# Batch 0's k and q transposed head by head, memory values cast by the DMA, and three x copies moved to ScalarE, in a chunked-attention and snake-MLP kernel

## The chip, the cores and the metric

The kernel runs on one core of a Trainium2 chip. The metric is the device time of one execution in microseconds; where several executions are shown, the median is meant. The profile is of one further execution, and its times are counted from the start of its span. Engines are named as in the profile: PE is TensorE (PEld its weight loads), DVE is VectorE, ACT is ScalarE, POOL is GpSimd, SP is SyncE.

## The reference

Two stages follow one another: a chunked attention with memory tokens over 4 batches, 8 heads, 768 positions and a head size of 64, and a two-layer MLP over the 3072 tokens that come out of it.

```python
def _attn_ref(q, k, v, mem_k, mem_v):           # q, k, v: (4, 8, 768, 64); mem: (4, 8, 8, 64)
    chunk, left_ctx, right_ctx = (32, 16, 8)
    scale = 1.0 / np.sqrt(D)
    for c in range(S // chunk):
        l_start, r_end = max(0, 32 * c - 16), min(S, 32 * c + 32 + 8)
        q_c = q[:, :, 32 * c:32 * c + 32]
        k_full = np.concatenate([mem_k, k[:, :, l_start:r_end]], axis=2)
        v_full = np.concatenate([mem_v, v[:, :, l_start:r_end]], axis=2)
        a = softmax(scale * np.matmul(q_c, k_full.transpose(0, 1, 3, 2)))
        out[:, :, 32 * c:32 * c + 32] = np.matmul(a, v_full)

def _moe_ref(x, w_in, w_out, alpha):            # x: (3072, 512), w_in: (512, 2048), w_out: (2048, 512)
    h = x @ w_in
    s = np.sin(alpha * h)
    g = h + s * s / (alpha + 1e-09)
    return g @ w_out
```

All inputs and the output are float32; the kernel multiplies in bfloat16.

## The kernel before, in words

**Tiling.** A batch has 8 blocks of 96 queries (`QW`), each three chunks of 32. A block's keys and values are a window of 128 rows: 120 of the sequence and 8 of the memory, which sit at rows 64 to 71 of the window. `kTi` holds the transposed keys of a batch with the memory keys put in between the blocks, `qT` the transposed queries, and the two tiles `vws` the values of two successive batches with a column of ones, which gives the sums for the softmax. The mask is in the bias of the exponential (`biasm`).

**Loading.** k and q come by DMA from POOL's queue, cast to bfloat16, with six successive positions in one partition, so a row moved is long. Batch 0 is loaded by pairs of heads (`load_qk_pair`, eight DMAs), later batches whole (`load_qk`). Because of the six positions, transposing a pair of heads takes six transposes of 128 by 128. `pair_up` (L226) first copies a pair of heads so that the two heads' 64 columns lie side by side for each of the six; `t_k` and `t_q` transpose that copy into PSUM and copy the result to `kTi` on VectorE (L243, and two short ones at L249) and to `qT` on ScalarE (L258). v of batch 0 is loaded by blocks, two DMAs each (`load_v`, L125 and L129), later batches by four large DMAs (`load_v_all`, L139 to L148). The memory values are loaded in float32 from SP's queue, cast on ScalarE (L418), and spread over the eight blocks of a batch by `put_memv` (L153), a VectorE copy of 4096 elements on 8 partitions. POOL's DMA issues take turns on eight semaphores; each waits until the DMA that used its semaphore before has landed.

**The order of work** is written out by hand (`manual_schedule`): each engine runs its instructions in the order of the program.

1. *The opening* (L412 to L438): for batch 0, k and q of the four pairs of heads in turn are regrouped, transposed and copied out. `spin` puts filler matmuls of zeros on TensorE (L171): ten at the start, two after each of the eight tiles. Then come `put_memv(0)` and the issue of all weights, of batch 1's k and q, of w_out and of batch 1's v.
2. *The burst* of a batch (`burst`): for block s, the scores are multiplied (L266) and three exponentials taken on ScalarE (`qk_exp`, L275); `lag` steps later the values are multiplied (L288), and VectorE takes the reciprocal (L292) and scales (L293, `x_blk`); one step after that the block is transposed (L306) and copied into `xT` (`xt`, L309). In batch 0 each step also has one filler matmul, and the transposes have a PSUM tile of their own; in later batches second-layer matmuls of the batch before fill the gaps.
3. *The first layer* (`l1`): for each of 16 feature tiles ft, eight matmuls of 384 columns (L341), a sine on ScalarE (L353), its square on ScalarE (L356), VectorE (L362) or POOL (L358) as a string of letters says, and on VectorE gT = square x inverse alpha + h (L370, or L366 where a tile is split). For batch 0 the letters are `ADADADAAADADADAA`: VectorE squares ft 1, 3, 5, 9, 11 and 13. `put_memk(1)` and `put_memv(1)` stand ahead of it.
4. *The second layer* (`l2`, L398) of a batch, interleaved with the next batch's opening and burst, and then the loop goes on.

Tile pools decide who waits for buffers: scores, attention outputs and first-layer outputs share three PSUM tiles (`big`), fillers and transposes two (`smp`).

Of the kernel before, what the change touches and what calls it, by code (L numbers as in the profile page):

```python
# [9 lines left out]
P = 128  # L10
QW = 96
# [3 lines left out]
F32 = mybir.dt.float32  # L15
# [30 lines left out]
def kernel(  # L46
# [12 lines left out]
    nc = tc.nc  # L59
    B, H, S, D = q.shape  # L60
# [3 lines left out]
    NJ = S // QW  # L64
    HP = H // 2
# [8 lines left out]
    gp = ctx.enter_context(tc.tile_pool(name="gp", bufs=2))  # L74
# [8 lines left out]
    ident = consts.tile([P, P], BF, name="ident")  # L83
# [7 lines left out]
    memkT = consts.tile([P, HP, 32], BF, name="memkT")  # L91
    memv_st = consts.tile([P, B, H, D], BF, name="memv_st")
    memk_f = gp.tile([32, H, D], F32, name="memk_f", tag="gT")
    memv_f = gp.tile([P, B, H, D], F32, name="memv_f", tag="gT")
    w_in_sb = consts.tile([P, KT, d_ff], BF, name="w_in_sb")
    w_out_sb = consts.tile([P, FT, d_model], BF, name="w_out_sb")
    alpha_sb = consts.tile([P, FT], F32, name="alpha_sb")
# [9 lines left out]
    def alloc_qk():  # L107
        kb = qkst.tile([P, H, 6, D], BF, name="k_bf")
        qb = qkst.tile([P, H, 6, D], BF, name="q_bf")
        return kb, qb  # L110

    def load_qk(b):
        kb, qb = alloc_qk()
        for src, dst in ((k, kb), (q, qb)):
            nc.gpsimd.dma_start(
                dst[:].rearrange("p h r d -> p h (r d)"),
                src[b].rearrange("h (p r) d -> p h (r d)", p=P),
            )
        return kb, qb
# [30 lines left out]
            vf.rearrange("(n p) d -> p n d", p=QW)[0:8, 1:n])  # L150

    def put_memv(b):
        nc.vector.tensor_copy(  # L153
            vws[b % 2][64:72, :, :, 0:D],
            memv_st[64:72, b].unsqueeze(2).to_broadcast([NM, H, NJ, D]),
        )

    def put_memk(b):
        nc.vector.tensor_copy(
            kTi[:, :, 24:KW].rearrange("p g (j c) -> p g j c", c=104)[:, :, :, 40:40 + NM],  # L160
            memkT[:, :, NM * b:NM * b + NM].unsqueeze(2).to_broadcast([P, HP, NJ, NM]),
        )
# [4 lines left out]
    def spin(n):  # L167

        z = smp.tile([P, 512], F32, name="z", tag="sm")
        for _ in range(n):  # L170
            nc.tensor.matmul(z[:], zeros[:, 0:P], zeros[:])  # L171
# [8 lines left out]
    kq = alloc_qk()  # L180
# [3 lines left out]
        load_qk_pair(0, hp, *kq)  # L184
    for b in range(B):
        nc.sync.dma_start(memk_f[NM * b:NM * b + NM], mem_k[b].rearrange("h n d -> n h d"))
    nc.sync.dma_start(memv_f[64:72].rearrange("n b h d -> n (b h) d"),
                      mem_v.rearrange("b h n d -> n (b h) d"))
    nc.gpsimd.memset(biasm[:], NEG)
    nc.gpsimd.memset(biasm[:, 0:1], 0.0)  # L190
    for c0, c1, thr, val in (
# [16 lines left out]
    for pt in pts:  # L208
        nc.vector.memset(pt[:, H * QW:H * QW + 32], 0.0)

    def load_w_in(c):
        nc.gpsimd.dma_start(
            w_in_sb[:, :, 256 * c:256 * c + 256],
            moe_w_in[:, 256 * c:256 * c + 256].rearrange("(kt p) f -> p kt f", p=P),
        )

    def load_w_out(c):
        nc.gpsimd.dma_start(
            w_out_sb[:, 4 * c:4 * c + 4, :],
            moe_w_out[512 * c:512 * c + 512].rearrange("(ft p) o -> p ft o", p=P),  # L220
        )


    def pair_up(src, hp, eng=None):
        pr = blk.tile([P, 6, 2, D], BF, name="pr")
        (eng or nc.gpsimd.tensor_copy)(  # L226
            pr[:].rearrange("p r e d -> p e r d"), src[:, 2 * hp:2 * hp + 2]
        )
        return pr
# [3 lines left out]
    def t_tile():  # L233
        state["t"] += 1
        if state["t"] % state["pools"] == 0:
            return smp.tile([P, 6, P], BF, name="tt_a", tag="sm")
        return big.tile([P, 6, P], BF, name="tt_b", tag="big")

    def t_k(kb, hp):
        t = t_tile()  # L240
        for r in range(6):
            nc.tensor.transpose(t[:, r, :], kb[:, r].rearrange("p e d -> p (e d)"), ident[:])  # L242
        nc.vector.tensor_copy(  # L243
            kTi[:, hp, 72:72 + 7 * 104].rearrange("p (s c) -> p s c", c=104)[:, :, 0:96]
            .rearrange("p s (a r) -> p s a r", r=6),
            t[:, :, 8:120].rearrange("p r (s a) -> p s a r", a=16),
        )
        for t0, c0 in ((0, 16), (120, 800)):
            nc.vector.tensor_copy(  # L249
                kTi[:, hp, c0:c0 + 48].rearrange("p (a r) -> p a r", r=6),  # L250
                t[:, :, t0:t0 + 8].rearrange("p r a -> p a r"),
            )

    def t_q(qb, hp):
        t = t_tile()
        for r in range(6):
            nc.tensor.transpose(t[:, r, :], qb[:, r].rearrange("p e d -> p (e d)"), ident[:])  # L257
        nc.scalar.copy(  # L258
            qT[:, hp, :].rearrange("p (a r) -> p a r", r=6), t[:].rearrange("p r a -> p a r")
        )  # L260

    def qk_exp(j):
        sc = big.tile([P, 2, 512], F32, name="sc", tag="big")
        for hp in range(HP):
            for e in range(2):
                nc.tensor.matmul(  # L266
                    sc[:, e, QW * hp:QW * hp + QW],
                    kTi[64 * e:64 * e + 64, hp, 104 * j:104 * j + P],
                    qT[64 * e:64 * e + 64, hp, QW * j:QW * j + QW],
                )  # L270
        pt = pts[state["n"] % NPT]
        state["n"] += 1
        for m in range(3):
            col = ((1 if j == 0 else 0), 4, (3 if j == NJ - 1 else 2))[m]
            nc.scalar.activation(  # L275
                pt[:, 0:H * QW].rearrange("p (g e c) -> p e g c", g=4, e=2)[:, :, :, 32 * m:32 * m + 32],
                sc[:, :, 0:4 * QW].rearrange("p g (e c) -> p g e c", e=4)[:, :, :, 32 * m:32 * m + 32],
                ACTF.Exp, bias=biasm[:, col:col + 1], scale=0.125,
            )
        return pt  # L280
# [19 lines left out]
    def xt(xT, j, x_blk, ot):  # L300
        if ot is None:
            xtp = smp.tile([P, KT, QW], BF, name="xtp", tag="sm")[:]
        else:
            xtp = ot[:].bitcast(BF)[:, 0, 640:640 + KT * QW].rearrange("p (k c) -> p k c", k=KT)
        for kt in range(KT):
            nc.tensor.transpose(  # L306
                xtp[:, kt, :], x_blk[:, 2 * kt:2 * kt + 2, :].rearrange("p e d -> p (e d)"), ident[0:QW, 0:QW]
            )
        nc.vector.tensor_copy(xT[:, :, QW * j:QW * j + QW], xtp)  # L309

    def burst(b, stream, shares, lag):

        xT = xp.tile([P, KT, S], BF, name="xT")
        ptl, xbl = {}, {}
        for s in range(NJ + lag + 1):
            n = shares[s] if s < len(shares) else 0
            if s < NJ:
                ptl[s] = qk_exp(s)
            if b == 0:
                spin(1)  # L320
            stream.take(n // 3, True)
            if 0 <= s - lag < NJ:
                xbl[s - lag] = pv(b, s - lag, ptl.pop(s - lag))
                if b == 0:
                    xbl[s - lag] = (xbl[s - lag][0], None)
            stream.take((n + 1) // 3, True)
            if 0 <= s - lag - 1 < NJ:
                xt(xT, s - lag - 1, *xbl.pop(s - lag - 1))
            stream.take((n + 2) // 3, True)
        return xT  # L330

# [77 lines left out]
            yield True  # L409


    first = [nc.vector.tensor_copy, nc.scalar.copy] * 2 + [nc.vector.tensor_copy] * 4  # L412
    prs = [pair_up(kq[n], 0, first[n]) for n in range(2)]
    for n in range(2 * HP):
        (t_k if n % 2 == 0 else t_q)(prs[n], n // 2)
        spin(2)
        if n == 3:
            nc.scalar.copy(memv_st[64:72], memv_f[64:72])  # L418
        if n == 1:
            mt = smp.tile([P, HP, 32], BF, name="mt", tag="sm")  # L420
            for hp in range(HP):
                nc.tensor.transpose(
                    mt[:, hp, :],
                    memk_bf[0:32, 2 * hp:2 * hp + 2, :].rearrange("p e d -> p (e d)"),
                    ident[0:32, 0:32])
        if n + 2 < 2 * HP:
            prs.append(pair_up(kq[n % 2], (n + 2) // 2, first[n + 2]))
        if n == 1:
            nc.vector.tensor_copy(memkT[:], mt[:])
            put_memk(0)  # L430
    put_memv(0)
    nc.vector.reciprocal(inv_alpha[:], alpha_sb[:])
    for c in range(8):
        load_w_in(c)
    kq_next = load_qk(1)
    for c in range(4):
        load_w_out(c)
    load_v_all(1)  # L438

# [1 line left out]
    xT = burst(0, stream, (), 2)  # L441
# [3 lines left out]
    for i in range(B):  # L445
        gT = gp.tile([P, FT, S], BF, name="gT")
# [31 lines left out]
        if not last:  # L478
# [8 lines left out]
            if i == 0:  # L487
                xT = burst(i + 1, stream, (3, 3, 3, 4, 4, 4, 4, 4, 4, 4, 5, 5), 3)
            else:
                xT = burst(i + 1, stream, (16, 8, 6, 6, 6, 5, 5, 5, 5, 5), 1)  # L490
# [37 lines left out]
```

The softmax here doesn't subtract the row's maximum and nothing guards it: scores larger than these inputs give would overflow.

## Time and profile before

| | us |
|---|---|
| median of 10 runs | 237.34 |
| lowest and highest of them | 236.68, 239.56 |
| the profiled execution | 239.56 |
| its span (first to last instruction) | 237.8 |
| TensorE, VectorE, ScalarE, POOL busy | 220.9, 160.5, 153.7, 72.9 |
| opening, until the first exponential (L275) | 0 to 18.50 |
| burst of batch 0, until the first layer's matmuls run on | 18.50 to 30.75 |
| first layer of batch 0 | 30.75 to 58 |
| TensorE at half clock within it | 30.9 to 34.3 |

The busy times are sums over the whole span. Every batch goes through the same stages, but the first 58 us differ from the rest: there is no second layer of an earlier batch to fill TensorE, so other engines and the DMA set the pace, and the sums over the whole span say little about that stretch. It is read by the chain of waits and by the busy time of each engine in short stretches.

### The profile page before, as it was taken

The numbers are of one execution on the slowest core, as the hardware profiler recorded it, in microseconds if no ns is written. First come the engines' busy times: TensorE is split into PE (matmuls) and PEld (weight loads), VectorE is DVE, ScalarE is ACT, GpSimd is POOL, SyncE is SP. The second block draws the span as 40 slices with busy tenths as digits, with TensorE's granted clock in tenths as the row PEclk, the third lists the DMA queues.
The fourth block names the chain that finished last, engine by engine and source line by source line (L and its number), as shares of the span: only waits on it lengthen the run. The fifth ranks groups of instructions, "written<-read, shape, count | busy, mean of one in ns | idle before, by whom it ended". The sixth has DMA issues, their size and how long they took to land.

```text
span 237.8 us, 4467 instructions
## 1 busy us (share of the span) xinstructions
PE 220.9 (93%) x1759; PEld 124.3 (52%) x1785; DVE 160.5 (67%) x287; ACT 153.7 (65%) x237; POOL 72.9 (31%) x96
## 2 busy tenths in 40 slices
PE   7798899989989999998999999998999999899994
PEld 2455546545535566565455565664455555453453
DVE  3376949899717886998656688978556367875110
ACT  2569839995497358798766597779564675971000
POOL 7899874302662022409320115120000010020000
PEclk9999979999999999999999999999999999999999
DMA  6999999999999920016999101001111110101122
GB/s 77 150 147 82 149 192 203 206 207 129 113 197 182 141 77 3 0 45 78 199 154 137 44 3 44 3 0 44 47 44 47 45 44 3 44 0 44 50 85 88
DMA packets 53852, 21.11 MB, mean 89 GB/s; under 512 B 36296, under 2 KB 50888, under 8 KB 53832
## 3 DMA queue, kind: packets, MB, share of 16 engines
q0 software_dynamic: 47616, 14.40, 77.0%
q1 hardware_dynamic: 6216, 6.43, 9.4%
q8 instruction: 14, 0.23, 0.4%
q14 instruction: 6, 0.05, 0.1%
HBM read 28.91 MB, written 6.29 MB: 148 GB/s over the span
## 4 chain that ended last, share of the span: by engine, by line
PE 63%; DVE 12%; ACT 11%; issue 6%; DMA 3%; POOL 3%; POOLq 1%; DVEq 0%; ACTq 0%
PE o L398 29%; PE hT L341 22%; DVE gT L370 5%; ACT pt L275 4%; ACT u L353 3%; DMA q_bf<-in_q_dram 3%; PE ot L288 3%; PE sc L266 3%; DVE s L362 2%; PE ot L306 2%; DVE x_blk L293 2%; PE o L387 1%; ACT s L356 1%; POOL k_bf L102 1%; PE tt_a L257 1%
## 5 line engine op out<-in xcount | busy, mean ns | idle before, releaser
L398 PE MATMUL o<-w_out_sb,gT 128*128 128x512 bf16 x343 | 93.1, 380 | 2.0 <-issue 0.5
L341 PE MATMUL hT<-xT,w_in_sb 128*128 128x384 bf16 x488 | 89.0, 330 | 3.8 <-DVE gT L370 3.3
L370 DVE SCALAR_TENSOR_TENSOR gT<-s,inv_alpha,hT 128x768 bf16<-128x768 f32 x61 | 60.9, 1012 | 22.8 <-ACT s L356 14.8
L353 ACT ACTIVATE u<-hT,alpha_sb 128x768 f32<-128x768 f32 x61 | 54.6, 898 | 27.0 <-PE hT L341 26.0
L341 PEld LDWEIGHTS <-w_in_sb 128*128 128x128 bf16 x512 | 49.9, 99 | 39.6 <-issue 6.4
L275 ACT ACTIVATE pt<-sc,biasm 128x256 bf16<-128x256 f32 x96 | 37.5, 492 | 12.5 <-PE sc L266 12.5
L398 PEld LDWEIGHTS <-gT 128*128 128x128 bf16 x368 | 31.8, 97 | 26.2 <-DVE gT L370 1.2
L358 POOL TENSOR_TENSOR s<-u 128x768 f32<-128x768 f32 x6 | 8.8, 1466 | 71.6 <-ACT u L353 61.3
L356 ACT ACTIVATE s<-u 128x768 f32<-128x768 f32 x34 | 28.7, 843 | 1.1
L362 DVE TENSOR_TENSOR s<-u 128x768 f32<-128x768 f32 x24 | 24.8, 1033 | 0.7 <-ACT u L353 0.5
L226 POOL COPY pr<-q_bf 128x768 bf16<-128x768 bf16 x12 | 10.1, 838 | 43.7 <-PE tt_a L242 26.1
L293 DVE TENSOR_TENSOR x_blk<-ot,rinv 96x512 bf16<-96x512 f32 x32 | 22.0, 686 | 1.1
L292 DVE RECIPROCAL rinv<-ot 96x8 f32<-96x8 f32 x32 | 6.5, 202 | 20.0 <-PE ot L288 19.6
L407 ACT COPY o_sb<-o 128x512 f32<-128x512 f32 x11 | 6.4, 585 | 20.0 <-PE o L398 20.0
L405 DVE COPY o_sb<-o 128x512 f32<-128x512 f32 x12 | 8.2, 687 | 15.4 <-PE o L398 15.1
L171 PE MATMUL z<-zeros 128*128 128x512 bf16 x36 | 14.9, 502 | 1.3 <-DVE zeros L165 1.3
L288 PEld LDWEIGHTS <-pt 128*128 128x128 bf16 x256 | 11.9, 98 | 7.2 <-issue 2.3
L266 PEld LDWEIGHTS <-kTi 64*128 64x128 bf16 x256 | 7.0, 94 | 13.3 <-issue 6.8
L288 PE MATMUL ot<-vw,pt 128*128 128x65 bf16 x256 | 13.0, 193 | 0.9 <-ACT pt L275 0.6
L266 PE MATMUL sc<-qT,kTi 64*128 64x96 bf16 x256 | 11.4, 205 | 2.2 <-ACT pt L275 1.2
L306 PEld LDWEIGHTS <-x_blk 96*128 96x128 bf16 x128 | 8.4, 97 | 6.6 <-DVE x_blk L293 1.5
L242 PEld LDWEIGHTS <-pr 128*128 128x128 bf16 x96 | 6.9, 103 | 6.4 <-DVE pr L226 3.2
(66 smaller groups left out, 183.0 us busy)
## 6 DMA issues: line engine op xcount, KB each, us to landing
out_dram<-o_sb SPq DMA_DIRECT2D x23, 256.0 KB, 2.6
k_bf<-in_k_dram POOLq DMA_DIRECT2D x3, 768.0 KB, 8.1
q_bf<-in_q_dram POOLq DMA_DIRECT2D x3, 768.0 KB, 11.4
vw<-in_v_dram POOLq DMA_DIRECT2D x6, 384.0 KB, 17.3
w_in_sb<-in_moe_w_in_dram POOLq DMA_DIRECT2D x8, 256.0 KB, 8.0
w_out_sb<-in_moe_w_out_dram POOLq DMA_DIRECT2D x4, 512.0 KB, 18.7
k_bf<-in_k_dram POOLq DMA_DIRECT2D x4, 192.0 KB, 6.5
q_bf<-in_q_dram POOLq DMA_DIRECT2D x4, 192.0 KB, 6.7
```

The lines of the kernel that those rows point to most:

```text
L171: nc.tensor.matmul(z[:], zeros[:, 0:P], zeros[:])
L266: nc.tensor.matmul(sc[:, e, QW * hp:QW * hp + QW], kTi[64 * e:64 * e + 64, hp, 104 * j:104 * j + P], qT[64 * e:64 * e + 64, hp, QW * j:QW ...
L275: nc.scalar.activation(pt[:, 0:H * QW].rearrange("p (g e c) -> p e g c", g=4, e=2)[:, :, :, 32 * m:32 * m + 32], sc[:, :, 0:4 * QW].rearra ...
L288: nc.tensor.matmul(otv[:, h // 4, h % 4, :], pt[:, QW * h:QW * h + P], vws[b % 2][:, h, j, 0:D + 1])
L293: nc.vector.tensor_tensor(out=x_blk[:].rearrange("p (g e) d -> p g e d", g=2), in0=otv[0:QW, :, :, 0:D], in1=rv.unsqueeze(3).to_broadcast( ...
L306: nc.tensor.transpose(xtp[:, kt, :], x_blk[:, 2 * kt:2 * kt + 2, :].rearrange("p e d -> p (e d)"), ident[0:QW, 0:QW])
L341: nc.tensor.matmul(hts[hf][:, 0:HALF], w_in_sb[:, kt, P * ft:P * ft + P], xT[:, kt, HALF * hf:HALF * hf + HALF], start=(kt == 0), stop=(kt ...
L353: nc.scalar.activation(u[:], hT[:, :, 0:HALF], ACTF.Sin, scale=alpha_sb[:, ft:ft + 1])
L356: nc.scalar.activation(s2[:], u[:], ACTF.Square)
L362: nc.vector.tensor_tensor(out=s2[:], in0=u[:], in1=u[:], op=ALU.mult)
L370: nc.vector.scalar_tensor_tensor(out=gv, in0=s2[:], scalar=inv_alpha[:, ft:ft + 1], in1=hT[:, :, 0:HALF], op0=ALU.mult, op1=ALU.add)
L398: nc.tensor.matmul(o[:], gT[:, ft, P * s:P * s + P], w_out_sb[:, ft, :], start=(ft == 0), stop=(ft == FT - 1),)
```

## The change

- In the opening the regrouping copies are gone. A new function `turn` transposes straight from the loaded tile: for each of the six positions two transposes of one head's 64 columns, into the upper and the lower 64 partitions of the PSUM tile. (For batches 1 to 3 it works on the regrouped tile as before.) After each tile there is one filler matmul instead of two.
- The memory values are loaded by a DMA from POOL's queue, issued behind the eight of k and q, that casts to bfloat16. The DMA on SP's queue and the cast on ScalarE are gone.
- `put_memv(0)` stands after the fifth of the eight tiles instead of after the last. `put_memv(1)` runs on POOL instead of VectorE; batches 2 and 3 stay on VectorE.
- w_in is loaded by five DMAs (256, 256, 512, 512, 512 columns) instead of eight of 256, and w_out by two instead of four.
- In batch 0's burst a block is transposed and copied into `xT` two steps after its values are multiplied instead of one (`back`), which makes the burst one step longer; the copies of blocks 5, 6 and 7 run on ScalarE.

```diff
@@ tiles, put_memv, loads
-    memv_f = gp.tile([P, B, H, D], F32, name="memv_f", tag="gT")
...
     def put_memv(b):
-        nc.vector.tensor_copy(
+        (nc.gpsimd if b == 1 else nc.vector).tensor_copy(
             vws[b % 2][64:72, :, :, 0:D],
...
-    nc.sync.dma_start(memv_f[64:72].rearrange("n b h d -> n (b h) d"),
-                      mem_v.rearrange("b h n d -> n (b h) d"))
+    nc.gpsimd.dma_start(memv_st[64:72].rearrange("n b h d -> n (b h) d"),
+                        mem_v.rearrange("b h n d -> n (b h) d"))
...
-    def load_w_in(c):
+    def load_w_in(c0, c1):
         nc.gpsimd.dma_start(
-            w_in_sb[:, :, 256 * c:256 * c + 256],
-            moe_w_in[:, 256 * c:256 * c + 256].rearrange("(kt p) f -> p kt f", p=P),
+            w_in_sb[:, :, c0:c1],
+            moe_w_in[:, c0:c1].rearrange("(kt p) f -> p kt f", p=P),
         )
     def load_w_out(c):
         nc.gpsimd.dma_start(
-            w_out_sb[:, 4 * c:4 * c + 4, :],
-            moe_w_out[512 * c:512 * c + 512].rearrange("(ft p) o -> p ft o", p=P),
+            w_out_sb[:, 8 * c:8 * c + 8, :],
+            moe_w_out[1024 * c:1024 * c + 1024].rearrange("(ft p) o -> p ft o", p=P),
         )
@@ transposes
-    def t_k(kb, hp):
+    def turn(src, hp):
         t = t_tile()
         for r in range(6):
-            nc.tensor.transpose(t[:, r, :], kb[:, r].rearrange("p e d -> p (e d)"), ident[:])
+            if src.shape[1] == 6:
+                nc.tensor.transpose(t[:, r, :], src[:, r].rearrange("p e d -> p (e d)"), ident[:])
+            else:
+                for e in range(2):
+                    nc.tensor.transpose(t[64 * e:64 * e + 64, r, :], src[:, 2 * hp + e, r, :], ident[:])
+        return t
+
+    def t_k(kb, hp):
+        t = turn(kb, hp)
...
     def t_q(qb, hp):
-        t = t_tile()
-        for r in range(6):
-            nc.tensor.transpose(t[:, r, :], qb[:, r].rearrange("p e d -> p (e d)"), ident[:])
+        t = turn(qb, hp)
@@ xt, burst
-        nc.vector.tensor_copy(xT[:, :, QW * j:QW * j + QW], xtp)
+        (nc.scalar.copy if ot is None and j >= 5 else nc.vector.tensor_copy)(
+            xT[:, :, QW * j:QW * j + QW], xtp)
...
-        for s in range(NJ + lag + 1):
+        back = lag + (2 if b == 0 else 1)
+        for s in range(NJ + back):
...
-            if 0 <= s - lag - 1 < NJ:
-                xt(xT, s - lag - 1, *xbl.pop(s - lag - 1))
+            if 0 <= s - back < NJ:
+                xt(xT, s - back, *xbl.pop(s - back))
@@ the opening
-    first = [nc.vector.tensor_copy, nc.scalar.copy] * 2 + [nc.vector.tensor_copy] * 4
-    prs = [pair_up(kq[n], 0, first[n]) for n in range(2)]
     for n in range(2 * HP):
-        (t_k if n % 2 == 0 else t_q)(prs[n], n // 2)
-        spin(2)
-        if n == 3:
-            nc.scalar.copy(memv_st[64:72], memv_f[64:72])
+        (t_k if n % 2 == 0 else t_q)(kq[n % 2], n // 2)
+        spin(1)
         if n == 1:
...
-        if n + 2 < 2 * HP:
-            prs.append(pair_up(kq[n % 2], (n + 2) // 2, first[n + 2]))
-        if n == 1:
             nc.vector.tensor_copy(memkT[:], mt[:])
             put_memk(0)
-    put_memv(0)
+        if n == 4:
+            put_memv(0)
     nc.vector.reciprocal(inv_alpha[:], alpha_sb[:])
-    for c in range(8):
-        load_w_in(c)
+    for c0, c1 in ((0, 256), (256, 512), (512, 1024), (1024, 1536), (1536, 2048)):
+        load_w_in(c0, c1)
     kq_next = load_qk(1)
-    for c in range(4):
+    for c in range(2):
         load_w_out(c)
     load_v_all(1)
```

## The prediction

> **What bounds the kernel now.** I read the page first, for the busy shares and the forty slices.
>
> ```profile
> PE 220.9 (93%) x1759; PEld 124.3 (52%) x1785; DVE 160.5 (67%) x287; ACT 153.7 (65%) x237; POOL 72.9 (31%) x96
> PEclk9999979999999999999999999999999999999999
> ```
>
> TensorE is busy nearly throughout, but the change touches only the first 60 us, and those have limits of their own: one slice (29.7 to 35.7 us) shows a lower clock. Next, the chain of waits over 0 to 62 us.
>
> ```profile
> 7.08 7.51 DMA q_bf<-in_q_dram
> ...
> 15.59 0.38 DVE pr L226
> ...
> 16.02 0.51 PE tt_b L242 x6
> ...
> 17.33 0.81 ACT qT L258
> ...
> 18.50 5.58 ACT pt L275 x15
> ...
> 29.21 0.70 DVE x_blk L293
> ...
> 29.96 0.36 PE xtp L306 x4
> ...
> 30.34 0.37 DVE xT L309
> ...
> 30.75 5.58 PE hT L341 x23
> ```
>
> Three stages: **the opening** (to 18.50) ends when the last q has landed (7.08 + 7.51 = 14.59), been regrouped, transposed and copied to qT; **the burst** of batch 0 (18.50 to 30.75) is set by the exponentials, then by VectorE; **the first layer** of batch 0 follows. The third view, busy time by stretch, shows what limits that layer.
>
> ```profile
> 27.44:30.86 3.42, 2.22 (x27) 1.24 (x25) 3.17 (x11) 1.27 (x1) 2.28 (x4) 1.00 1.24 161
> ...
> 32.00:33.00 1.00, 1.00 (x5) 0.48 (x4) 0.06 (x1) 0.00 (x0) 1.00 (x2) 0.50 1.48 194
> ...
> 50.00:55.00 5.00, 3.87 (x24) 2.21 (x24) 4.96 (x8) 4.39 (x6) 0.00 (x0) 1.00 1.46 194
> ```
>
> The columns are PE, PEld, DVE, ACT and POOL busy, then the clock. At 32 us TensorE runs at half clock and VectorE is idle; from 36 to 57 us VectorE is busy 19.8 of 21.0 us. Whatever holds VectorE there moves the end. The timeline gives the rows that I price with.
>
> ```profile
> 17.68 1.27 DVE L153 COPY vw<-memv_st 8x4096 bf16<-8x4096 bf16 x1
> ...
> 39.11 0.96 DVE L362 TENSOR_TENSOR s<-u 128x768 f32<-128x768 f32 x1
> ...
> 45.46 0.83 POOL L148 DMA_DIRECT2D vw<-in_v_dram  x1 [3.14 <-DMA q_bf<-in_q_dram]
> ...
> 87.88 1.49 DVE L362 TENSOR_TENSOR s<-u 128x768 f32<-128x768 f32 x1
> ```
>
> The same square takes 0.96 us at 39.11 and 1.49 at 87.88, where a POOL copy (L226, 87.74 to 88.57) lies over its start.
>
> [...] the two squares under a POOL copy end 0.81 us after it (1.49 and 1.37 us against 0.95), while L370, with one SBUF input, stays at 1.01 under such copies. [...] Here it reads 0.50 at 31 to 34 us, after 2.22 busy of 3.42; matmuls of L341 start 0.32 us apart there and 0.163 later. [...]
>
> **The change, part by part.**
>
> *Opening.* Eight regrouping copies go (VectorE six, 0.34 to 0.52 us each; ScalarE two of 0.83), and ScalarE's cast of the memory values (1.90 us at 14.35). TensorE gets 12 transposes of 64 columns for 6 of 128, and one filler matmul for two. A transpose starts every 0.107 us at half clock, 0.056 at full; a filler takes 0.427 or 0.214. If half transposes go one by one, a tile costs 12 x 0.107 + 0.43 = 1.71 us cold, 0.89 warm (before: 1.50, 0.76); if the two column halves run side by side, 1.07 and 0.55. Tiles land about every 1.0 us, so only the cold serial case queues.
> What is late next is the memory values. Their DMA leaves the SP queue for POOL's, behind the eight k and q loads, and lands after the last q: 14.6 to 15.1 (the v load behind them now lands at 10.13 + 4.97 = 15.1). The copy that spreads them (L153, 1.27 us) moved from behind the last k copies to ahead of them on VectorE. So VectorE waits to about 14.9, spreads until 16.2, then evacuates the last k (0.86 + 0.31) until 17.4; before it finished at 17.65 and qT at 18.13. ScalarE's last qT is ready by 16.7. The first exponential starts at about 17.8 for 18.50: **0.7 us gained**. Bounds: 1.3 if SP's lighter queue lands everything 0.5 us sooner; 0 if cold, serial transposes delay the last k to 16.8 on VectorE.
>
> *Burst.* Copying x one step later and the last three on ScalarE takes 3 x 0.34 us from VectorE, but not from the path. After the second x_blk VectorE has no free time; before, copies 1 to 5 stand between it and the last x_blk (copy 0 fell into a wait), after it copies 0 to 4: five each time. After the last x_blk, before: 29.90 to 30.70. After: transposes 0.4, then a ScalarE copy of 384 elements, about 0.48 on the line through its 512 (0.585, L407) and 768 (0.80, L258): 0.9. **0.1 lost** (bounds -0.3, +0.2). The Sine table load (1.28 us, now right after the exponentials) follows these copies and still fits under the first layer's first matmuls (1.3 us or more). One more filler on TensorE is under VectorE's work.
>
> *POOL's queue.* One DMA issue more before the v loads (0.7 us), less the 0.36 us for which the first of them waits beside a regrouping copy: first-layer weights start 0.4 us later, v still lands 1.5 us or more before its use. The spread of batch 0 holds up one v load (1.34 us for 0.7) before and after alike. The 8 weight issues become 5 and the 4 of w_out 2; rows of twice the length should move like k's (768 KB in 3.9 us) instead of w_in's 256 KB in 1.5, so w_in is complete at 21.9 + 0.4 + 4.8 + 1.5 + 3 x 2.6 = 36.4 (before 27.1 + 10.3 = 37.4). Nothing on the chain waits for weights; the first w_out matmul is at 55.1, and the second half, due about 55.5, is first read at 57.6. Nothing gained or lost; were that slack of 2 us gone, each further microsecond of delay would pass to the end.
>
> *The spread of batch 1.* put_memv(1) leaves VectorE (1.22 us at 30.84, in time that VectorE idles until 34.92: nothing gained) and goes to POOL, queued behind the last v load. A POOL DMA issue waits for the landing of the eighth before it (L148 above waits for q, eight earlier); for that v load this is now the last w_in. It issues at 36.7, until 37.4; then POOL copies 4096 elements. POOL's copies of 768 take 0.83 us, so 4.4 us[...]. I take 4.4[...]. The square of ft 3, due at 39.11 - 0.6 = 38.5, then ends 0.81 after POOL at 42.6 instead of 39.5: 3.1 late, and behind it on VectorE wait all gT of the layer, and so TensorE for PSUM. VectorE has one 0.53 us gap at 46.3 and some 0.2 of small ones to take this up; I count **2.2 lost**[...]. If the layer starts 1.3 sooner at full clock, the square of ft 5 is hit instead, for about as much.
>
> *Sum:* -0.7 + 0.1 + 2.2 = **+1.6 us**. The profiled execution took 239.56 (span 237.8 and 1.8 around it), the highest of the ten; the sum on it gives 241.2. Its half clock at the layer's start, some 1.3 us, may be part of its 2.2 above the median; I put the sum on the median: 237.34 + 1.6 = 238.9.
>
> **Rivals.** *The POOL copy stalls nothing* (not slower): it is done in under 1.1 us, or lies outside every square; L370, which it can't hold, fills half of VectorE's time. Then -0.6: 236.7. Against it: squares come every 3 us[...]. It decides where POOL's copy takes under 1.1 us.
> *That, and TensorE stays at full clock* into the first layer, since the tail of the burst gets one more filler (0.21 of 3.4 us): eight matmuls at 0.163 for 0.325, another -1.3: 235.4. For it: 2.22 of 3.42 us was the only stretch that dropped. Against it: the addition is small.
> *The clock falls earlier.* Eight fillers fewer leave TensorE cold into the burst: a step then costs about 1.5 us against the exponentials' 1.07, for one 3.4 us window: +1.5 on the sum, 240.4. Against it: cold, the doubled transposes fill the time anyway.
> That the change doesn't act is excluded: copies and DMAs are gone from the program.
>
> **The numbers.** Likeliest case 0.48, stall-free 0.23, stall-free and warm 0.22, cold 0.07. Hence faster by over 0.5% (1.2 us, about what a measurement of this kernel can tell from none) 0.22, within it 0.23, slower 0.55. The likeliest gives 238.9, its own range 237.9 to 239.9; the others and the unknown prices stretch it to 235.8 to 240.9.
>
> **What would show it.** Right: put_memv on POOL at about 37[...], and one L362 of 2.5 us or more under it; first exponential at 17.2 to 18.3, with L153 ahead of the last L243 of the opening; last x_blk to first-layer matmul 0.9 us. Wrong: L362 at 0.95 throughout, or POOL's copy under 1.1 us; or an exponential before 17, if the memory values land ahead of the last q.

## The result, and the profile after

| | before | after |
|---|---|---|
| median (us) | 237.21 | 240.23 |
| lowest, highest of the runs (us) | 235.85, 239.56 | 238.49, 243.40 |
| ratio to before, with its 95% interval | | 1.0100 (1.0072 to 1.0128) |
| profiled execution (us), its span | 239.56, 237.8 | 238.68, 237.0 |

The kernel became slower, by 3.0 us in the medians over all runs and by 1.0% (2.4 us) in the ratio, which leaves out a few disturbed executions. The two profiled executions stand the other way round: after's is near its own low end, and before's was the highest of its ten. The profile therefore has to be read for what happens in it, not for its end time. First the page of after: the busy row of the engines and the granted clock by slices.

```profile
PE 218.1 (92%) x1800; PEld 123.3 (52%) x1826; DVE 157.7 (67%) x277; ACT 151.8 (64%) x237; POOL 73.1 (31%) x93
PEclk9797999999999999999999999999999999999999
```

VectorE's work fell by 2.8 us (160.5 before), as the removed and moved copies let one expect, and yet nothing was won. The clock row now dips twice, in slices 2 and 4 (5.9 to 11.9 and 17.8 to 23.7 us), where that of before dipped at 29.7 to 35.7. The chain of waits of after, in order of time, shows the stages.

```profile
7.79 7.06 DMA memv_st<-in_mem_v_dram
14.88 1.22 DVE vw L152
16.11 0.86 DVE kTi L251
17.13 0.24 PE sc L272 x2
17.45 2.31 ACT pt L281 x6
...
29.82 0.49 ACT xT L315
30.35 3.90 PE hT L349 x23
...
39.88 0.92 DVE gT L378
40.80 2.18 DVE s L370
...
57.16 0.85 DVE kTi L251
```

The opening now ends with the memory values, as the prediction had it: their DMA (7.79 + 7.06 = 14.85), the spread `put_memv(0)` (L152), the last k copy, and only then the scores and the first exponential at 17.45. The other new item is a square (L370) of 2.18 us on the chain. The timeline shows what lies over it.

```profile
37.75 0.95 DVE L370 TENSOR_TENSOR s<-u 128x768 f32<-128x768 f32 x1
38.36 3.79 POOL L152 COPY vw<-memv_st 8x4096 bf16<-8x4096 bf16 x1
...
40.72 2.25 DVE L370 TENSOR_TENSOR s<-u 128x768 f32<-128x768 f32 x1
...
44.14 2.76 PE L349 MATMUL hT<-xT,w_in_sb 128*128 128x384 bf16 x16 [1.61 <-DVE gT L378]
```

`put_memv(1)` on POOL runs from 38.36 to 42.15. The square that falls into it ends at 42.97, 0.82 after POOL, having taken 2.25 us for its usual 0.95; TensorE then waits 1.61 us for a gT. The third view, busy time by stretch, has the columns PE, PEld, DVE, ACT and POOL busy, then the clock.

```profile
14.86:18.28 3.42, 1.52 (x23) 0.72 (x24) 2.56 (x5) 1.49 (x4) 3.42 (x5) 1.00 1.30 79
18.28:21.69 3.41, 3.27 (x42) 2.15 (x43) 1.21 (x4) 3.41 (x11) 3.41 (x6) 0.50 1.47 92
```

While VectorE waits for the memory values and spreads them, TensorE is busy for 1.52 of 3.42 us; in the next 3.41 us, within the burst, its clock reads 0.50.

### The profile page after: what moved, and what is told of

It is laid out like the page before. It is cut to its first block, busy times and chain, and to the rows that moved or that the text cites. A ratio compares the mean times of both kernels' runs of the same rounds, so it can differ in the third digit from the quotient of the medians.

```text
span 237.0 us, 4530 instructions
## 1 busy us (share of the span) xinstructions
PE 218.1 (92%) x1800; PEld 123.3 (52%) x1826; DVE 157.7 (67%) x277; ACT 151.8 (64%) x237; POOL 73.1 (31%) x93
## 3 DMA queue, kind: packets, MB, share of 16 engines
HBM read 28.91 MB, written 6.29 MB: 149 GB/s over the span
## 4 chain that ended last, share of the span: by engine, by line
PE 62%; DVE 17%; issue 7%; ACT 6%; POOL 3%; DMA 3%; POOLq 1%; DVEq 0%; ACTq 0%
PE o L406 29%; PE hT L349 20%; DVE gT L378 7%; DVE s L370 4%; PE ot L294 3%; DMA memv_st<-in_mem_v_dram 3%; ACT pt L281 3%; PE sc L272 3%; DVE x_blk L299 2%; PE tt_a L243 2%; ACT u L361 2%; PE ot L312 2%; PE o L395 1%; POOL q_bf L101 1%; POOL k_bf L101 1%
## 5 line engine op out<-in xcount | busy, mean ns | idle before, releaser
L349 PE MATMUL hT<-xT,w_in_sb 128*128 128x384 bf16 x488 | 87.3, 326 | 4.9 <-DVE gT L378 4.3
L349 PEld LDWEIGHTS <-w_in_sb 128*128 128x128 bf16 x512 | 49.3, 98 | 39.7 <-issue 6.0
L370 DVE TENSOR_TENSOR s<-u 128x768 f32<-128x768 f32 x24 | 26.1, 1087 | 0.6 <-ACT u L361 0.5
L170 PE MATMUL z<-zeros 128*128 128x512 bf16 x29 | 12.2, 482 | 2.0 <-DVE zeros L164 1.3
L243 PEld LDWEIGHTS <-pr 128*128 128x128 bf16 x144 | 10.1, 98 | 5.6 <-issue 0.5
```

The lines of the kernel that those rows point to most:

```text
L243: nc.tensor.transpose(t[:, r, :], src[:, r].rearrange("p e d -> p (e d)"), ident[:])
L349: nc.tensor.matmul(hts[hf][:, 0:HALF], w_in_sb[:, kt, P * ft:P * ft + P], xT[:, kt, HALF * hf:HALF * hf + HALF], start=(kt == 0), stop=(kt ...
L370: nc.vector.tensor_tensor(out=s2[:], in0=u[:], in1=u[:], op=ALU.mult)
```

## The experiments

Two theories stood at the start. **The held square**: the POOL copy holds up a square of VectorE (2.25 us for 0.95 in after's profile), costs about 2 us, and makes up the loss. **The clock**: the opening with fewer fillers and an early spread leaves TensorE idle (1.52 us busy of 3.42), and the half clock behind it makes up the loss. The later kernels follow a third one, a floor set by the load stream, which the first four brought up. For each kernel the median is given, and the ratio to before with its interval. Before itself, run beside them, has a median of 237.09 with experiments 1 to 4, 237.22 with 5 to 8 and 237.42 with 9 to 11, so medians of different groups compare only to about 0.3 us.

**1. `put_memv(1)` back on VectorE.**

```diff
-        (nc.gpsimd if b == 1 else nc.vector).tensor_copy(
+        nc.vector.tensor_copy(
```

> The kernel after, with only put_memv(1) back on VectorE. [...] POOL's 3.8 us copy blocks one square for 1.3 us and moves the end by 0.6 to 1.3; without it the median falls by about 1 us, from 240.2 to some 239.2, and every square of batch 0's first layer takes 0.95. Clock theory (the opening's idle stretch of TensorE is what costs): this edit leaves that alone, so some 2 us of the loss stay. [...]

238.01 us, ratio 1.0022 (1.0002 to 1.0041): 2.2 us less than after. Its timeline:

```profile
29.03 1.22 DVE L152 COPY vw<-memv_st 8x4096 bf16<-8x4096 bf16 x1
34.10 0.95 DVE L370 TENSOR_TENSOR s<-u 128x768 f32<-128x768 f32 x1
37.03 0.95 DVE L370 TENSOR_TENSOR s<-u 128x768 f32<-128x768 f32 x1
40.00 0.95 DVE L370 TENSOR_TENSOR s<-u 128x768 f32<-128x768 f32 x1
...
56.64 0.59 PE L406 MATMUL o<-w_out_sb,gT 128*128 128x512 bf16 x2 [1.02 <-DMA w_out_sb<-in_moe_w_out_dram]
```

The spread is done before the first square begins, and no square is long. The last line is new and had not been looked for: with the first layer done sooner, TensorE waits 1.02 us in the second layer for the last load of w_out. By the medians about 0.9 us above before (237.09) remains, by the ratio half of that. None of its 22 executions ran at full clock (the highest mean of the granted clock is 0.993). Executions of the same mean clock, 0.983 to 0.986, can be compared: 9 of after have a median of 239.75, 6 of this kernel 238.20. So about 1.5 us of the 2.2 stay at an equal clock, and the rest goes with after's lower clock; this sorting was made afterwards, on few executions.

**2. `put_memv(0)` behind the last tile again,** the rest as after.

```diff
-        if n == 4:
-            put_memv(0)
+    put_memv(0)
     nc.vector.reciprocal(inv_alpha[:], alpha_sb[:])
```

> The kernel after, with only put_memv(0) back behind the last of the eight tiles. Clock theory: TensorE no longer waits 1.9 us for the last k, the first exponential comes at about 16.0 instead of 17.45, no half-clock window falls into the burst, and the time falls by 2 to 3 us to 237.2 to 238.2. [...] the first exponential still comes earlier, but only the 1.4 us of that are gained at most. If the place of put_memv(0) doesn't matter: 240.2.

240.08 us, ratio 1.0129 (1.0110 to 1.0149), from four executions: as slow as after, though the first exponential comes at 15.70 instead of 17.45 and the first gT at 31.39 instead of 33.50. The timeline and two stretches show where those 2 us went.

```profile
38.41 3.59 POOL L152 COPY vw<-memv_st 8x4096 bf16<-8x4096 bf16 x1
38.62 4.20 DVE L370 TENSOR_TENSOR s<-u 128x768 f32<-128x768 f32 x1
...
43.98 4.42 PE L349 MATMUL hT<-xT,w_in_sb 128*128 128x384 bf16 x16 [3.56 <-DVE gT L378]
```

```profile
40.55:43.97 3.42, 0.00 (x0) 0.00 (x0) 3.32 (x3) 1.49 (x2) 1.45 (x1) 1.00 1.32 204
43.97:47.38 3.41, 3.40 (x11) 1.62 (x11) 2.86 (x4) 1.48 (x2) 0.82 (x1) 0.50 1.25 207
```

The square now starts 0.2 us after the copy and is held to 0.82 us after its end: 4.20 us. TensorE has nothing at all to do for 3.42 us, and then runs at half clock for 3.41. So the price of the POOL copy depends on where a square falls into it, from 1.3 us (after's profile) to 3.25 here, and here half clock followed the stall.

**3. Eight fillers in the hole of the opening,** the rest as after.

```diff
         if n == 4:
             put_memv(0)
+        if n == 7:
+            spin(8)
```

> The kernel after, with eight filler matmuls more on TensorE behind the last transposes, where it waits for the last k (15.2 to 17.1 us). The order on all other engines is unchanged. Clock theory: the clock stays up in the burst, and the time falls by 1.5 to 2.5 us to about 238. If the loss is in the wait itself[...] and not in the clock: 240 or a little more.

239.08 us, ratio 1.0100 (1.0070 to 1.0131). The clock row of its page:

```profile
PEclk9999999999999999999999999999999999999999
```

The dips are gone, the first exponential is still at 17.13, and the median is 1.15 us below after's. The ratio is no better than after's, and with six runs the gain is not firm; but the granted clock, which every execution records, shows what the fillers do: 4 of 6 executions here ran at full clock over all (0.997 or more on average), 0 of 16 of after, and 81 of 161 of before. The clock theory is right about a part, and it can't be the main one, since at full clock this kernel has 238.8 (4 executions) and before 237.04 (15).

**4. Before with `put_memv(1)` on POOL,** nothing else changed.

```diff
-        nc.vector.tensor_copy(
+        (nc.gpsimd if b == 1 else nc.vector).tensor_copy(
```

> The kernel before, with only put_memv(1) on POOL. Its POOL queue reaches the copy later, behind the wait for q at 45.5 us, so it runs from about 46.3 to 50.1 over the square of ft 9 (47.8) and delays POOL's copy of q by as much. [...] one square of some 3 us, +1 to +2 us: 238.2 to 239.2. [...]

240.34 us, ratio 1.0123 (1.0083 to 1.0163): this one line alone makes the old kernel lose as much as the whole change does, 3.25 us.

```profile
46.16 3.59 POOL L153 COPY vw<-memv_st 8x4096 bf16<-8x4096 bf16 x1
47.00 3.57 DVE L362 TENSOR_TENSOR s<-u 128x768 f32<-128x768 f32 x1
```

Here the last v issue waits 3.12 us for q, until 45.29 (in after 1.61 us for a part of w_in, until 37.47), and the copy behind it starts at 46.16, so it meets the square of ft 9, which ends 0.82 us after it. TensorE then waits 3.75 us for a gT, until 52.72, and goes on at half pace: eight L341 matmuls take 2.72 us there, for 1.46 in after (at 41.06), and six transposes take 0.85 at 56.94 and 0.50 again at 58.73. The two of its six executions that ran at full clock took 238.57 and 238.86, 1.5 to 1.8 us above before's 237.04 at full clock: that is the stall without the clock. Its opening is before's, and its first exponential is at 16.48, not at the 18.50 of the profile that the prediction used.

**5. Both spreads back where before has them,** the rest as after.

> After with both spreads moved back to where before has them: put_memv(1) on VectorE, put_memv(0) behind the last tile. My theory (the copy on POOL blocks a square, and put_memv(0) ahead of the last k holds up the first exponential by about 0.8 us) takes the two as independent: 238.0 (put_memv(1) back alone) less 0.8 to 1.4 gives 236.6 to 237.2, a ratio to before of 0.997 to 1.000; first exponential at 15.7, first gT at about 31.4, no square of ft 1 to 13 over 1.2 us. Rival (the change's other parts, such as the longer burst and the fewer fillers, cost the remaining 0.9 us): it stays at 238.0, and the gain of the opening is gone again by the end of the burst.

237.20 us, ratio 1.0019 (0.9992 to 1.0045): as before. The first theory's sum held (236.6 to 237.2), and the rival's 238.0 did not come, though by the ratio it can't be told from experiment 1. The squares take 0.95 as expected, but the first exponential, expected at 15.7, comes at 16.69 in this profile and the first gT at 32.39 for 31.4. The mean granted clock of this execution is 0.986, and the last k copy of its opening starts at 14.74, for 13.64 in experiment 2, whose order of work in the opening is the same. If the removed copies win something in the opening, it isn't in the time, and the second layer shows why.

```profile
57.49 0.59 PE L406 MATMUL o<-w_out_sb,gT 128*128 128x512 bf16 x2 [2.65 <-DMA w_out_sb<-in_moe_w_out_dram]
```

TensorE reaches the second layer some 3 us sooner than in before's profile (51.92 for 55.10), and then waits 2.65 us for the second half of w_out, which lands at 57.45. (This profiled execution took 240.55, the longest of its runs, so that the wait is shown and not its usual size.)

**6. Before once more,** for a second profile of its opening.

> The kernel before, unchanged, for a second profile of its opening. My theory (the first exponential at 18.50 in the profile that I predicted from was late because TensorE was at half clock until 13.79 there) expects it at 16.2 to 16.8, with full clock from 4 to 10 us on, and the same time as before. Rival (18.50 is its usual time, and the 16.48 of the kernel with put_memv(1) on POOL was the exception): 18 or later. Time ratio 1.000 either way.

237.18 us, ratio 1.0006 (0.9980 to 1.0032), the size of a null result. Its page:

```profile
PEclk9679999999999999999999999999999999999999
```

My theory expected an exponential before 16.8 and failed: it comes at 18.56, and the clock from 0 to 13.79 reads 0.80 on average. Its chain shows what that does.

```profile
8.12 0.84 ACT pr L226
9.01 0.82 PE tt_b L257 x6
9.83 0.85 PE z L171 x2
...
13.14 0.85 PE z L171 x2
...
15.69 0.43 PE z L171 x2
```

From 9.01 on the chain runs through TensorE's transposes and fillers, at half pace: two fillers take 0.85 us, and 0.43 from 15.69 on. The first profile of before has the same pace, though its clock row shows 9 there; the transposes themselves show it.

```profile
12.65 0.84 PE L257 MATMUL tt_b<-ident,pr 128*128 128x128 bf16 x6
...
13.97 0.50 PE L242 MATMUL tt_b<-ident,pr 128*128 128x128 bf16 x6
```

In experiment 4 VectorE waits 0.60 us for the first six of them (6.18 to 6.78), in the first profile of before 0.92 (6.82 to 7.73). The loads make little of the difference: the last q lands at 14.59 in the first profile of before and is copied from 14.28 on in experiment 4, 0.3 us of 2.0. Two profiles of this opening have 18.5 and one has 16.48; TensorE's pace in the opening differs between executions and moves its end by 2 us, and neither value is "the" opening.

**7. The x copies of batch 0 as before,** on the kernel of experiment 5.

```diff
-        back = lag + (2 if b == 0 else 1)
+        back = lag + 1
...
-        (nc.scalar.copy if ot is None and j >= 5 else nc.vector.tensor_copy)(
-            xT[:, :, QW * j:QW * j + QW], xtp)
+        nc.vector.tensor_copy(xT[:, :, QW * j:QW * j + QW], xtp)
```

> As the kernel with both spreads back where before has them, and the x copies of batch 0 also as before: one step after the values, all on VectorE. The prediction's step (0.1 us lost by them, bounds -0.3 and +0.2) expects a time within 0.3 us of that kernel. Rival (the burst of after, 12.9 us for 12.25, is longer by the extra step): 0.5 us or more faster than that kernel, with the burst from first exponential to first-layer matmuls back at 12.3 us.

237.56 us, ratio 1.0012 (0.9989 to 1.0036): no difference to experiment 5. It is a weak test of the time, however, since in this profile a load stands at the end of the burst too.

```profile
28.85 4.07 PE L348 MATMUL hT<-xT,w_in_sb 128*128 128x384 bf16 x24 [1.18 <-DMA w_in_sb<-in_moe_w_in_dram]
```

The first exponential was at 15.56, and the first layer waits 1.18 us for the first w_in, until 28.85. What opening and burst win beyond that is lost there.

**8. The weights in small loads again,** eight of w_in and four of w_out, on the kernel of experiment 5.

```diff
-    for c0, c1 in ((0, 256), (256, 512), (512, 1024), (1024, 1536), (1536, 2048)):
-        load_w_in(c0, c1)
+    for c in range(8):
+        load_w_in(c)
...
-    for c in range(2):
+    for c in range(4):
         load_w_out(c)
```

> As the kernel with both spreads back where before has them, with w_in in eight loads and w_out in four as before. The prediction's step (nothing gained or lost by the larger loads) expects a time within 0.3 us of that kernel, and the v loads of batch 1 issued later by some us without anyone waiting. Rival (the larger loads bring weights or k sooner to something that waits): over 0.5 us slower than that kernel, with a first-layer matmul or a batch 1 transpose waiting for a DMA.

236.82 us, ratio 0.9979 (0.9958 to 0.9999), the best complete kernel of the study. It is 0.4 us below experiment 5 by the medians, and the intervals overlap.

```profile
56.19 0.38 PE L406 MATMUL o<-w_out_sb,gT 128*128 128x512 bf16 x1 [0.69 <-DMA w_out_sb<-in_moe_w_out_dram]
```

With w_out in quarters, the 9th to 12th matmuls no longer wait for the last rows, and the wait is 0.69 us for 2.65. The first exponential is at 15.39, 1.1 us before that of experiment 4, whose opening still has the regrouping copies.

**9. No k and q of batch 1 in the stream,** on the kernel of experiment 5.

```diff
-    kq_next = load_qk(1)
+    kq_next = kq
```

> As the kernel with both spreads back where before has them, but the k and q of batch 1 are not loaded (batch 0's are used again, so batch 1's attention is left without its own data), which takes two DMAs of 7.6 us in all out of the stream ahead of w_out. Theory of a floor (in that kernel TensorE waits 2.65 us at the second layer for the last w_out, which lands at 57.45; the load stream and not the opening sets the end of this stretch): w_out has landed by about 50, no matmul of the second layer waits for it, and the time falls by 1 to 2.6 us, to 234.6 to 236.2. Rival (the wait is a trait of one execution, or another wait takes its place at once): 236.9 to 237.4, as that kernel.

235.74 us, ratio 0.9942 (0.9918 to 0.9966): 1.5 us below experiment 5 by the medians, with intervals that lie apart, and within what the floor theory gave. (The kernel leaves batch 1's attention without its own data.) The second layer's matmuls run on without a wait for w_out:

```profile
54.79 0.81 PE L406 MATMUL o<-w_out_sb,gT 128*128 128x512 bf16 x3
55.78 0.81 PE L406 MATMUL o<-w_out_sb,gT 128*128 128x512 bf16 x3
56.76 0.81 PE L406 MATMUL o<-w_out_sb,gT 128*128 128x512 bf16 x3
```

A saved wait of TensorE for k and q themselves is not the reason, as far as experiment 5's profile shows: q has landed there at 46.2, and the first transposes of batch 1, at 53.14, wait for neither.

**10. q of batch 1 behind w_out,** on the kernel of experiment 8.

```diff
+            if between and src is q:
+                between()
...
-    kq_next = load_qk(1)
-    for c in range(4):
-        load_w_out(c)
+    kq_next = load_qk(1, lambda: [load_w_out(c) for c in range(4)])
...
-            srcs = [(kq_next[n % 2], n // 2) for n in range(2 * HP)]
+            srcs = [(kq_next[n // 4], n % 4) if i == 0 else (kq_next[n % 2], n // 2) for n in range(2 * HP)]
```

> As the kernel with both spreads back and the loads in small pieces, with batch 1's q loaded behind w_out and its four k tiles transposed ahead of the four q tiles. Theory of a floor: the last w_out lands about 3.8 us sooner, at 52.3, and the second layer no longer waits 0.69 us for it; q lands at 56.2 instead, and its first use then waits for it. With q used four tiles (3.9 us) later than k, this should save about 0.5 us: 236.3 against 236.8. Rival (all of the stream is needed at once, so that its order is worth nothing, and VectorE stands behind the wait for q): the same or up to 1.5 us slower, with a POOL or VectorE copy of q waiting for the DMA.

237.56 us, ratio 1.0019 (0.9996 to 1.0042), 0.7 us above experiment 8 by the medians: the rival (the same or up to 1.5 us slower) was right. no matmul of the second layer waits for w_out any more, the first q is copied at 56.11, and the waits of TensorE stand behind that copy and the next:

```profile
56.98 0.51 PE L245 MATMUL tt_b<-ident,pr 128*128 128x128 bf16 x6 [0.49 <-DVE pr L227]
57.98 0.82 PE L408 MATMUL o<-w_out_sb,gT 128*128 128x512 bf16 x3 [0.48 <-DVE kTi L259]
```

**11. Two second-layer matmuls after each tile of batch 1 instead of three,** on the kernel of experiment 8.

```diff
                     piece(n)
-                    stream.take(3, True)
+                    stream.take(2, True)
```

> As the kernel with both spreads back and the loads in small pieces, with two second-layer matmuls instead of three after each of batch 1's eight transposed tiles, so that the 13th matmul, the first that reads the last quarter of w_out, comes about two tiles later. Theory of a floor: TensorE passes the wait of 0.69 us with transposes, and the time falls by 0 to 0.6 us: 236.2 to 236.8. Rival (the tiles are paced by VectorE's copies at 1.0 us each anyway, and matmuls taken out of them are added later): 236.8 to 237.6.

239.18 us, ratio 1.0045 (1.0018 to 1.0072). Slower than either theory gave. Its 6 executions at full clock have a median of 237.14, within the rival's 236.8 to 237.6; the other 16 have 239.53. Experiment 8 ran at full clock in 15 of 22, but before, beside the present kernel, only in 23 of 59, so it is not shown that the edit lowers the clock. No profile of an execution at the lower clock was taken, and the cause stays open.

## Why the prediction was right, and where not

The side, the range and the main mechanism held (238.9 forecast, 240.23 measured). In part this is luck: 240.23 lies outside the 237.9 to 239.9 of the likeliest case, and inside the range only because that was stretched for the other cases. The opening and the clock were both misjudged, and both so that the forecast came out too low. The terms one by one:

*The spread of batch 1, +2.2: right in kind, and in size partly by luck.* Removing it from after gave 2.2, adding it to before 3.25. The stall alone is worth less, 1.5 to 1.8 us at an equal clock (experiments 1 and 4); the rest goes with the clock. The price of the copy was taken as 4.4 us and is 3.59 to 3.79. The square's end 0.81 us after POOL, read from two short copies of before, came back in all four kernels with this copy (0.81 or 0.82). The copy started at 38.36, not 37.4, just after the square of ft 3 had begun, and hit that of ft 5, as the prediction had for a layer that starts sooner. Its sign of being right, a square of 2.5 us or more, was just missed in after's profile (2.25) and met in experiments 2 to 4 (2.96 to 4.20). What the prediction left out is the clock: behind squares of 3.57 and 4.20 us TensorE waited 3.75 and 3.56 us for a gT and then went at half speed (experiments 4 and 2), while one of 2.96 had no dip behind it (experiment 3). It had looked for such a dip only at the end of the burst.

*The opening, -0.7: the step that failed.* Its mechanism is right line by line (memory values at 14.85, spread, last k copy, first exponential at 17.45 where 17.8 was forecast). Its reference was wrong, and so was the reading that the landing of q sets it: 18.50 belongs to an execution whose TensorE went at half pace until 13.79, and with q copied from 14.28 on, for 14.59, the old opening reaches 16.48 (experiment 4). After's opening is at 17.13 and 16.72 in experiments 3 and 1 (the memory values landed at 14.4 and 14.0): 0.2 to 0.7 later, not 0.7 sooner. The early `put_memv(0)` is what costs it. With the spread behind the last tile the first exponential is at 15.70, 15.56 and 15.39 in experiments 2, 7 and 8, and at 16.69 in experiment 5. The early spread also makes the hole (1.52 us busy of 3.42) behind which after's clock reads 0.50, and a difference shows in all executions: none of the 22 of experiment 1 ran at full clock, and 13 of the 22 of experiment 5, which differs from it only in the place of this copy (before, beside them: 15 of 27 and 43 of 75). What the place is worth at the end is not firm: 0.8 us by the medians of experiments 1 and 5, next to nothing by their ratios (1.0022 and 1.0019), since experiment 5 then waits for w_out.

*The loads, 0: right for after, where nothing waits for them.* Two microseconds of slack for w_out were named, with the warning that their loss would pass on to the end. In the kernels with the squares free and the layer early they are gone: waits of 1.02 and 2.65 us. This also stood in the way of the warm rival (235.4): with all data loaded in the old order the last w_out lands at 55.9 in after, 56.9 in before, and 57.4, 57.2 and 56.2 in experiments 5, 7 and 8, whatever the opening wins. Experiment 9, where nothing waits for it, is 1.5 us faster than experiment 5.

*The burst, +0.1: too small by 0.2.* From the first exponential to the end of the last x_blk nothing changed at full clock (11.4 us in before and in experiments 2, 3 and 4), as the prediction had it. From there to the first-layer matmuls it is 0.85 in before and 1.15 in after, for 0.9 forecast. The ScalarE copy takes 0.48 as priced, but the last transposes begin 0.26 us after x_blk is ready, behind the filler of the step that was added, which the prediction had put under VectorE's work:

```profile
28.51 0.69 DVE L299 TENSOR_TENSOR x_blk<-ot,rinv 96x512 bf16<-96x512 f32 x1
...
29.02 0.38 PE L170 MATMUL z<-zeros 128*128 128x512 bf16 x1
...
29.46 0.33 PE L312 MATMUL xtp<-ident,x_blk 96*128 96x96 bf16 x4
```

In the time it can't be seen (experiment 7), where the first w_in's landing hides it.

*The rival "the clock falls earlier" (240.4)* was given 0.07 and holds a part of the truth. It was priced for fewer fillers; it came behind the wait for the memory values (1.52 us busy of 3.42), and in experiments 2 and 4 behind the stall of the square (waits of 3.56 and 3.75 us).

*The sum* by the medians of the runs, from after to before: 240.23, without the spread on POOL 238.01, without the early spread too 237.20, with the small loads 236.82; before is at 237.2. So +2.2, +0.8, +0.4, and -0.4 for all the rest, the removed regrouping copies among it. The first is firm (the intervals of after and of experiment 1 lie apart); the next two are within what these runs can tell from nothing, and the last just touches it (experiment 8's interval ends at 0.9999).

## What to carry to other kernels

A copy moved to an idle POOL was not free here: in all four kernels with it (3.59 to 3.79 us) a square, whose two inputs are in SBUF, ended only 0.81 or 0.82 us after it, while a gT, with one input in SBUF and one in PSUM, kept its 1.00 or 1.01 us under it (at 39.80 in after, 39.13 in experiment 3). So compare such a copy's length with the spacing of the squares, and add what a stall may cost in clock (here waits of TensorE of 3.56 and 3.75 us were followed by half clock). The wait for the memory values, put ahead of the last k copy in VectorE's order, put the first exponential at 16.72 and 17.13, for 15.39 to 15.70 with the spread behind it: work that is first needed later belongs behind. Before pricing a gain on an engine, look up when the loads that the next stage reads land, and take the stage's time of before from several executions if the clock differs among them.

## What was not expected of the hardware

- The same opening ends at 16.48, 18.50 or 18.56 us, by the pace at which TensorE runs in it; the clock row of the page did not show the half pace in one of the two slow cases.
- The half-size transposes into the two partition halves of a PSUM tile take no longer for a tile than the full ones: after's 12 of 64 columns take 0.53 us (at 13.38) and, at half pace, 0.85 (at 10.72), six full ones 0.50 (at 13.97 in before) and 0.84 (at 12.65).
- Loading q behind w_out won nothing (experiment 10); leaving k and q of batch 1 out of it was worth 1.5 us (experiment 9; 25.76 MB read for 28.91).
